# Five small moves in the attention half of a fused attention and feed-forward kernel

## The chip, the cores and the metric

The kernel runs on one core of one Trainium2 chip. The metric is the device time of one launch in microseconds (us). The core has five engines that run side by side, each through its own list of instructions in order, and wait for each other by semaphores: TensorE (PE; its weight loads are shown as PEld), VectorE (DVE), ScalarE (ACT), GpSimd (POOL) and SyncE (SP), which here does nothing but issue DMA transfers. TensorE writes to PSUM, and DVE and ACT read it from there.

## The reference

```python
scores = q @ k.T / 8 + bias[head]          # 4 batches, 8 heads, 576 x 576, head size 64
attn = exp(scores - max); attn = attn / (sum(attn) + 1e-9)
x = (attn @ v) as (2304, 512)
x = max(x @ w1, x @ w2, x @ w3) @ w_out    # 512 -> 768 -> 512
h = x @ w_in                               # 512 -> 2048
out = where(h > 0, h, exp(min(h, 0)) - 1) @ w_out2
```

The bias is a small network of the two positions, one 576 x 576 table per head, the same for all batches. The inputs are 32-bit floats; the weights of the feed-forward parts arrive as 64-bit floats and are taken apart by integer operations on the chip.

## The kernel before

It has three parts. A prologue (to about 56 us) computes the bias tables and writes them to DRAM. The attention part follows (to about 317 us). The rest is the two feed-forward layers, in which TensorE is busy without a break.

The attention part handles 16 pairs n of two heads of one batch. A pair has five steps c: steps 0 to 3 take 128 queries of both heads each, step 4 takes the last 64 queries of both heads at once. So there are 80 steps, s = 5n + c. The steps are staggered: a table of numbers (`OFF`, `PV_AT`, `X_AT`) gives each piece of work of step s a key such as s + 2.10. All pieces are sorted by key, and emitted in that order. I call "slot c" the stretch of keys in which the scores of a step c are made. Keys do not set times: each engine runs its own pieces in the order of their keys as soon as their semaphores allow.

What happens in slot s, on each engine, in order:

- PE: scores of the first head of step s into PSUM tile PB[0] (`unit_qk`, L222), of the second head into PB[1]; then the turning of step s-2 (`trans`, L252), which turns the exponentials of 512 keys per head, in 64 x 64 pieces, into the PSUM tiles TQ[0] and TQ[1] by a matmul with a diagonal matrix of the reciprocal sums; then the tails (`tails`, L252 too), the same for the last 64 keys, into columns at the two ends of PB[0]; then some products with v (`pv`, L319 to L327) into the PSUM tiles XO[0] and XO[1]. Step 4 has one score tile and half as much to turn.
- DVE: `scores` of the first head (L230, reads PB[0], adds the bias, keeps the minimum; its second instruction, READ_ACCUMULATOR, ends it); the sum plus 1e-9 and its reciprocal for step s-1 (L240, L241); `scores` of the second head; the copy of the tails out of PB[0] (L77, `p<-pb`); one operation of the weight decoder (`pump`, L420 to L430; not in slot 1); the copy of TQ[1] for steps 0 and 2, the steps named by `EVD` (L77, `p<-tq`).
- ACT: the exponentials (L235), the other copies of TQ (L75), and the copy of XO[0] (`x_copy`, L341). DVE adds XO[1] to it (`x_sum`, L345).
- POOL: the diagonal matrices (`diag`, L249), one instruction per head, and the split of the result into a high and a low part (L73, L81).
- SP: per pair one load of q and k (`load_kq`, L96, 864 KB), one of v (`load_v`, L100, 320 KB), in every fourth pair nine loads of bias, and about one load of raw weights (L371) and one store of split weights (L466) per pair. Each waits in order until its buffer is free. There are two buffers for q and k, and two for v.

Of the kernel before, what the change touches and what calls it, by code (L numbers as in the profile page):

```python
# [31 lines left out]

OFF = {"qk0": 0.0, "qk1": 0.01, "t0": 0.02, "ns": 1.025, "dg": 1.026, "t1": 0.03, "tr": 2.10, "tl": 2.20, "evt": 2.311,
       "pump": 0.32, "ev0": 2.385, "ev1": 2.387, "ex0": 0.38, "ex1": 0.40}
PV_AT = {1: [(4.5, 0), (4.5, 1), (5.5, 2), (5.5, 3), (5.5, 4)],
         4: [(3.5, 0), (3.5, 1), (4.5, 2), (4.5, 3), (5.5, 4)]}
X_AT = {1: 5.6, 4: 5.6}
EVD = {0, 2}  # L40
# [13 lines left out]
def fused_kernel(ctx, tc, tkq, vv, lt, pk, wm1, wo1, win2, wo2, out):  # L54
    nc = tc.nc
# [29 lines left out]
    tp = att.enter_context(tc.tile_pool(name="tp", bufs=2))  # L85
    sp = att.enter_context(tc.tile_pool(name="sp", bufs=8))
# [3 lines left out]
    kq = att.enter_context(tc.tile_pool(name="kq", bufs=2))  # L90

    KQ, TV = {}, {}

    def load_kq(n):
        KQ[n] = kq.tile([128, 1728], F32, tag="kq", name="kq_t")
        nc.sync.dma_start(KQ[n], tkq[n])  # L96

    def load_v(n):
        TV[n] = ld.tile([128, 640], F32, tag="tv", name="tv_t")
# [21 lines left out]
    with ExitStack() as pro:  # L121
# [18 lines left out]
        with tc.manual_schedule():  # L140
            nc.sync.dma_start(pk_t, pk)
            nc.sync.dma_start(lt_t[:, 512:1148], lt[:, 512:1148])
            nc.sync.dma_start(lt_t[:, 0:512], lt[:, 0:512])
            load_kq(0)
            load_v(0)
            nc.vector.tensor_scalar(nbt, psi_t, b1_t, -1.0, op0=ALU.mult, op1=ALU.mult)
# [32 lines left out]
            for A in range(36):  # L179
# [9 lines left out]
                o = bt.tile([128, 576], F32, tag="o", name="o_t")  # L189
# [5 lines left out]
                c, r = divmod(A, 8)  # L195
# [11 lines left out]
    TQ, XO = [[psp.tile([128, 512], F32, name=f"{n}{i}") for i in range(2)] for n in ("tq", "xo")]  # L207
    PAIR = [(PB[i][:, 0:512], PB[i][:, 512:1024]) for i in (1, 0)] + [tuple(TQ), tuple(XO)]
    ident2 = xp.tile([128, 64], F32, name="ident2")
    nc.vector.tensor_copy(ident2[0:64], ident[0:64, 0:64])  # L210
    nc.vector.tensor_copy(ident2[64:128], ident[64:128, 64:128])
    H64 = [slice(0, 64), slice(64, 128)]
    steps = [(n, c) for n in range(4 * NP) for c in range(5)]
    E, ST, PT = {}, {}, {}
# [19 lines left out]
        e, st = E[s][:, 576 * h:576 * h + 576], ST[s]  # L234
        nc.scalar.activation(e, e, AF.Exp, bias=st[:, h:h + 1], scale=-1.0, accum_out=st[:, 2 + h:3 + h])  # L235

    def recip(s):
        nh = 2 if steps[s][1] < 4 else 1
        st = ST[s]
        nc.vector.tensor_scalar(st[:, 4:4 + nh], st[:, 2:2 + nh], 1e-9, None, op0=ALU.add)  # L240
        nc.vector.reciprocal(st[:, 6:6 + nh], st[:, 4:4 + nh])  # L241

    DG = {}

    def diag(s):
        nh = 2 if steps[s][1] < 4 else 1
        DG[s] = sp.tile([128, 2, 64], F32, tag="dg", name="dg_t", bufs=3)
        for h in range(nh):
            nc.gpsimd.tensor_scalar(DG[s][:, h], ident2, ST[s][:, 6 + h:7 + h], 1.0, op0=ALU.mult, op1=ALU.mult)  # L249

    def flip(dst, s, g, h, k0):
        mm(dst, E[s][H64[g], k0:k0 + 64], DG[s][H64[g], h % nheads(s)], start=True, stop=True)  # L252

    def nheads(s):
        return 2 if steps[s][1] < 4 else 1
# [14 lines left out]
            for h in range(2):  # L270
                flip(x[h][0:64], s, h, 0, 512)

    def trans(s):
        n, c = steps[s]
        if c == 0:
            PT[n, 0] = [tp.tile([128, 8, 256], F32, tag="pa", name="p0", bufs=1)]
        elif c == 2:
            PT[n, 1] = [tp.tile([128, 8, 320], F32, tag="pc", name="p1", bufs=1)]
        if c in (0, 2):
            PT[n, c // 2].append(tp.tile([128, 256], F32, tag="p3", name="p3", bufs=3))  # L280
        elif c == 4:
            PT[n, 1].append(tp.tile([64, 128], F32, tag="p4", name="p4", bufs=1))
        for h in range(nheads(s)):
            for k in range(4):
                for g in range(2):
                    for kh in range(2):
                        col = 256 * h + 64 * k
                        flip(TQ[g][H64[kh], col:col + 64], s, g, h, 576 * h + 128 * k + 64 * kh)
# [41 lines left out]
    XF = {}  # L330

    def x_where(s):
        n, c = steps[s]
        hp, b = divmod(n, 4)
        w, t0 = (256, b * S) if c == 1 else (320, b * S + 256)
        return XH[:, hp, t0:t0 + w], XL[:, hp, t0:t0 + w], w

    def x_copy(s):
        w = x_where(s)[2]
        XF[s] = tp.tile([128, 320], F32, tag="xf", name="xf", bufs=1)[:, 0:w]  # L340
        nc.scalar.activation(XF[s], XO[0][:, 0:w], AF.Copy)  # L341

    def x_sum(s):
        w = x_where(s)[2]
        nc.vector.tensor_tensor(out=XF[s], in0=XO[1][:, 0:w], in1=XF[s], op=ALU.add)  # L345

    def x_hi(s):
        hi_of("p", x_where(s)[0], XF[s])
# [199 lines left out]
    def at(key, fn, *args):  # L548
        plan.append((key, len(plan), fn, args))

    for s, (n, c) in enumerate(steps):
        o = {nm: s + off for nm, off in OFF.items()}
        at(o["qk0"], unit_qk, s, 0)
        at(o["t0"], scores, s, 0)
        at(o["ex0"], expo, s, 0)
        if c < 4:
            at(o["qk1"], unit_qk, s, 1)
            at(o["t1"], scores, s, 1)
            at(o["ex1"], expo, s, 1)
# [139 lines left out]
    def small(tag, bufs):  # L699
        return mp.tile([128, NB], F32, tag=tag, name=f"{tag}_t", bufs=bufs)  # L700
# [61 lines left out]
    with tc.manual_schedule():  # L762
        for n, u in enumerate(units + [None]):
# [6 lines left out]
            if n < 2:  # L770

                for i in range(2):
                    w = take_w(("wi", u[1], 3 * i))
                    v = take_w(("w3", pre[1], i)) if pre else None
                    for q, (b, d) in enumerate(((B11, B21), (B12, B22))):
# [3 lines left out]
                        c = small("c", 4)  # L779
# [14 lines left out]
            w = take_w(("wi", u[1], 0))  # L794
# [11 lines left out]
            w = take_w(("wi", u[1], 1))  # L806
# [11 lines left out]
            w = take_w(("wi", u[1], 2))  # L818
# [10 lines left out]
            w = take_w(("wi", u[1], 3))  # L829
# [71 lines left out]
```

## Time and profile before

| | us |
|---|---|
| median of 3 runs (1012.16 to 1016.56) | 1013.38 |
| the profiled execution | 1010.22 |
| its span from the first to the last instruction | 1008.4 |
| PE busy in the span | 977.4 (97%) |
| DVE, ACT, POOL busy | 692.1, 526.1, 341.7 |

The profile is of one execution. Its times count from the start of the span. A busy PE can still be a PE that has waited, since the ends of matmuls are modelled: two starts far apart tell more than a small idle time. "<- X" names what an idle engine waited for; "issue" is idle time in which it waited for nothing that the profile shows.

### The profile page before, as it was taken

How to read it: one execution, taken by the hardware profiler on the slowest of the kernel's cores; microseconds unless marked ns; L12 is line 12 of the kernel's file. 1: busy time of each engine (PE TensorE's matmuls, PEld its weight loads, DVE VectorE, ACT ScalarE, POOL GpSimd, SP SyncE). 2: the span in 40 equal slices, each digit the busy share in tenths (PEclk: the TensorE clock that was granted, in tenths of full speed). 3: DMA queues.
4: the chain of work that ended last, by engine and by line, in shares of the span. 5: the costliest groups of instructions: out<-in, count | busy, mean ns of one | idle time of the engine just before them, and what ended most of it. 6: DMA issues, size and time to landing. Idle time of an engine off the chain costs nothing.

```text
span 1008.4 us, 28525 instructions
## 1 busy us (share of the span) xinstructions
PE 977.4 (97%) x11748; PEld 869.2 (86%) x11748; DVE 692.1 (69%) x1428; ACT 526.1 (52%) x1087; POOL 341.7 (34%) x419
## 2 busy tenths in 40 slices
PE   7979899999999999999999999999999999999998
PEld 4447777778887899999999999998998989988996
DVE  7967778788886699887887862835574355743342
ACT  8967777777775233333333331644445344453443
POOL 0013344344343354534553550323232132321222
PEclk9989999999999999999999999999999999999999
DMA  7842724645532356879886981355657556575553
GB/s 259 291 172 85 247 94 157 205 163 187 176 127 79 134 187 215 308 234 341 321 282 236 328 298 47 116 189 175 199 192 252 191 171 204 188 258 185 176 197 105
DMA packets 65905, 201.00 MB, mean 199 GB/s; under 512 B 7024, under 2 KB 14832, under 8 KB 65776
## 3 DMA queue, kind: packets, MB, share of 16 engines
q1 hardware_dynamic: 65776, 199.18, 57.6%
q8 instruction: 93, 1.52, 0.6%
q14 instruction: 36, 0.29, 0.1%
HBM read 150.78 MB, written 48.37 MB: 197 GB/s over the span
## 4 chain that ended last, share of the span: by engine, by line
PE 91%; DVE 6%; issue 1%; DMA 1%; ACT 0%; SPq 0%; POOL 0%; DVEq 0%; POOLq 0%; ACTq 0%
PE xo L696 18%; PE pb L740 13%; PE pb L526 12%; PE tq L740 6%; PE tq L252 6%; PE xo L319 6%; PE xo L526 5%; PE tq L526 5%; PE pb L222 5%; PE pb L620 4%; PE pb L183 3%; PE pbb L183 2%; DVE e_t L230 2%; PE xo L620 2%; PE tq L620 2%
## 5 line engine op out<-in xcount | busy, mean ns | idle before, releaser
L81 POOL TENSOR_TENSOR gl<-t_t,gh 128x384 fp32r<-128x384 f32 x96 | 108.7, 1142 | 286.3 <-ACT gh L75 286.3
L235 ACT ACTIVATE e_t<-e_t,st_t 128x576 f32<-128x576 f32 x144 | 111.4, 773 | 58.6 <-DVE st_t L240 56.1
L230 DVE CUSTOM_DVE_ANT_0 e_t<-pb,b_t 128x576 f32<-128x576 f32 x144 | 107.7, 749 | 32.7 <-PE pb L222 32.5
L249 POOL TENSOR_SCALAR dg_t<-ident,st_t 128x64 f32<-128x64 f32 x144 | 48.1, 348 | 212.7 <-DVE st_t L241 93.2
L740 PE MATMUL pb<-w_t,gh 128*128 128x512 f32 x384 | 119.3, 392 | 0.0
L526 PE MATMUL pb<-xh,w_t 128*128 128x384 f32 x448 | 116.8, 336 | 0.0
L252 PEld LDWEIGHTS tq<-dg_t,e_t 64*64 64x64 f32 x4608 | 96.6, 136 | 22.7 <-issue 7.7
L252 PE MATMUL tq<-dg_t,e_t 64*64 64x64 f32 x4608 | 97.8, 222 | 10.9 <-issue 5.3
L696 PE MATMUL xo<-tt,w_t 128*128 128x384 f32 x528 | 107.4, 338 | 0.0
L718 ACT ACTIVATE t_t<-c_t 128x384 f32<-128x384 f32 x96 | 50.0, 521 | 103.4 <-DVE c_t L709 95.6
L222 PE MATMUL pb<-kq_t 64*64 64x288 f32 x1152 | 98.6, 413 | 3.8 <-issue 1.3
L696 PEld LDWEIGHTS xo<-tt,w_t 128*128 128x128 f32 x528 | 95.0, 188 | 7.7 <-issue 0.3
L696 PE MATMUL xo<-xh,w_t 128*128 128x384 f32 x328 | 94.6, 335 | 0.0
L319 PE MATMUL xo<-p,tv_t 64*64 64x320 f32 (+1 forms) x1024 | 85.4, 408 | 1.6 <-issue 1.2
L526 PEld LDWEIGHTS pb<-xh,w_t 128*128 128x128 f32 x448 | 81.1, 188 | 0.5 <-issue 0.4
L740 PEld LDWEIGHTS pb<-w_t,gh 128*128 128x128 f32 x384 | 70.5, 188 | 6.6
L740 PE MATMUL pb<-w_t,gl 128*128 128x512 f32 x192 | 75.5, 393 | 0.0
L526 PE MATMUL pb<-xl,w_t 128*128 128x384 f32 x224 | 75.3, 336 | 0.0
L75 ACT ACTIVATE p<-tq 128x512 f32<-128x512 f32 (+1 forms) x128 | 62.8, 528 | 16.4 <-PE tq L252 15.2
L222 PEld LDWEIGHTS pb<-kq_t 64*64 64x64 f32 x1152 | 50.9, 133 | 22.9 <-DVE p L77 4.4
L75 ACT ACTIVATE gh<-t_t 128x384 fp32r<-128x384 f32 x96 | 48.6, 519 | 33.4 <-DVE t_t L726 33.4
L696 PEld LDWEIGHTS xo<-xh,w_t 128*128 128x128 f32 x328 | 60.2, 188 | 3.0
(131 smaller groups left out, 2198.1 us busy)
## 6 DMA issues: line engine op xcount, KB each, us to landing
w_t<-scw_w SPq DMA_DIRECT2D x90, 512.0 KB, 4.4
w_t<-scw_wi SPq DMA_DIRECT2D x74, 512.0 KB, 4.2
kq_t<-tkq SPq DMA_DIRECT2D x16, 864.0 KB, 5.4
scw_wi<-sp SPq DMA_DIRECT2D x26, 512.0 KB, 4.7
scw_w<-sp SPq DMA_DIRECT2D x22, 512.0 KB, 5.5
raw<-wo SPq DMA_DIRECT2D x22, 512.0 KB, 3.7
scr<-o_t SPq DMA_DIRECT2D x36, 288.0 KB, 3.9
raw<-wm SPq DMA_DIRECT2D x18, 512.0 KB, 4.1
```

The source lines that it names most:

```text
L75: nc.scalar.activation(dst, src, AF.Copy)
L81: e.tensor_tensor(out=dst, in0=src, in1=hi.bitcast(F32), op=ALU.subtract)
L183: mm(p[32 * a4:32 * a4 + 32, 224 + 288 * hf:512 + 288 * hf], w28, FT[A, a4][:, 288 * hf:288 * hf + 288], start=True, stop=True)
L222: mm(PB[h][H64[g], 224 + 288 * r:512 + 288 * r], t[H64[r], 576 + 576 * a + q0:640 + 576 * a + q0], t[H64[r], 288 * a:288 * a + 288], start ...
L230: nc.vector.tensor_tensor_reduce(out=E[s][:, 576 * h:576 * h + 576], in0=PB[h][:, 224:800], in1=BT[n // 4, c, h], op0=ALU.add, op1=ALU.min ...
L235: nc.scalar.activation(e, e, AF.Exp, bias=st[:, h:h + 1], scale=-1.0, accum_out=st[:, 2 + h:3 + h])
L252: mm(dst, E[s][H64[g], k0:k0 + 64], DG[s][H64[g], h % nheads(s)], start=True, stop=True)
L319: mm(XO[g][H64[h], 0:w], v[H64[g], 128 * k + 64 * h:128 * k + 64 * h + 64], ps[0][H64[g], 4 * h + k, :], start=(k == 0), stop=(k == 3 and ...
L526: mm(ps[blk][:, 0:NB], wt[:, ks], xt[:, kk, t0:t0 + NB], start=(j == 0), stop=(j == 11))
L620: mm(ps[blk][:, 0:NB], WO[0][:, kk, wt, ms], xt[:, bs], start=(j == 0), stop=(j == 3 * NM1 - 1))
L696: mm(ps, w[wt][:, ks], b[xt][:, kk], start=(start and j == 0), stop=(stop and j == 5), skip_group_check=True)
L740: mm(acc[t], g[:, ts], w[k], start=(f == 0 and i == 0 and j == 0), stop=(f == NU - 1 and i == 1 and j == 2))
```

## The change

Five edits, all in the attention part.

1. `diag` makes both diagonal matrices of a step in one VectorE instruction, right behind the reciprocal, instead of one GpSimd instruction per head.
2. `x_copy` copies XO[0] and also XO[1] on ACT, and `x_sum` adds the two copies on GpSimd.
3. `trans` is split by head, and `tails` stands between the two halves (keys 2.10, 2.11, 2.12, where the tails had 2.20). Step 4 has the first half alone.
4. The load of q and k becomes three of 288 KB each (k; q of the first head; q of the second) at keys one step apart, and all loads of q, k and v have keys one step later.
5. `EVD` has step 3 too: its copy of TQ[1] moves from ACT to DVE.

```diff
-OFF = {"qk0": 0.0, "qk1": 0.01, "t0": 0.02, "ns": 1.025, "dg": 1.026, "t1": 0.03, "tr": 2.10, "tl": 2.20, "evt": 2.311,
+OFF = {"qk0": 0.0, "qk1": 0.01, "t0": 0.02, "ns": 1.025, "t1": 0.03, "tr0": 2.10, "tl": 2.11, "tr1": 2.12, "evt": 2.311,
-EVD = {0, 2}
+EVD = {0, 2, 3}
...
-    def load_kq(n):
-        KQ[n] = kq.tile([128, 1728], F32, tag="kq", name="kq_t")
-        nc.sync.dma_start(KQ[n], tkq[n])
+    def load_kq(n, i=None):
+        if not i:
+            KQ[n] = kq.tile([128, 1728], F32, tag="kq", name="kq_t")
+        cs = slice(576 * i, 576 * i + 576) if i is not None else slice(0, 1728)
+        nc.sync.dma_start(KQ[n][:, cs], tkq[n][:, cs])
...
-        DG[s] = sp.tile([128, 2, 64], F32, tag="dg", name="dg_t", bufs=3)
-        for h in range(nh):
-            nc.gpsimd.tensor_scalar(DG[s][:, h], ident2, ST[s][:, 6 + h:7 + h], 1.0, op0=ALU.mult, op1=ALU.mult)
+        d = DG[s] = sp.tile([128, 2, 64], F32, tag="dg", name="dg_t", bufs=3)
+        nc.vector.tensor_tensor(out=d[:, 0:nh], in0=ident2.unsqueeze(1).to_broadcast([128, nh, 64]),
+                                in1=st[:, 6:6 + nh].unsqueeze(2).to_broadcast([128, nh, 64]), op=ALU.mult)
...
-        XF[s] = tp.tile([128, 320], F32, tag="xf", name="xf", bufs=1)[:, 0:w]
-        nc.scalar.activation(XF[s], XO[0][:, 0:w], AF.Copy)
+        XF[s] = [tp.tile([128, 320], F32, tag=f"xf{i}", name="xf", bufs=1)[:, 0:w] for i in range(2)]
+        for i in range(2):
+            nc.scalar.activation(XF[s][i], XO[i][:, 0:w], AF.Copy)
...
-        nc.vector.tensor_tensor(out=XF[s], in0=XO[1][:, 0:w], in1=XF[s], op=ALU.add)
+        nc.gpsimd.tensor_tensor(out=XF[s][0], in0=XF[s][0], in1=XF[s].pop(), op=ALU.add)
+        XF[s] = XF[s][0]
...
-        at(o["ns"], recip, s)
-        at(o["dg"], diag, s)
-        at(o["tr"], trans, s)
+        at(o["ns"], diag, s)
+        at(o["tr0"], trans, s, 0)
+        if c < 4:
+            at(o["tr1"], trans, s, 1)
         at(o["tl"], tails, s)
...
-        at(5 * n + 0.2, load_kq, n + 1)
-        at(5 * n + 6.2, load_v, n + 1)
+        for i in range(3):
+            at(5 * n + 1.2 + i, load_kq, n + 1, i)
+        at(5 * n + 7.2, load_v, n + 1)
```

TensorE's order at the tails of a full step: `tq_859` and `tq_860` are TQ[0] and TQ[1], `pb_99` is PB[0]. Before, the end of the turning, the tails, and the products with v:

```order
L252 MATMUL tq_859<-dg_t,e_t 64x64 x2
L252 MATMUL tq_860<-dg_t,e_t 64x64 x2
L252 MATMUL tq_859<-dg_t,e_t 64x64 x2
L252 MATMUL tq_860<-dg_t,e_t 64x64 x2
L252 MATMUL pb_99<-dg_t,e_t 64x64 [waits DVE_49]
L252 MATMUL pb_99<-dg_t,e_t 64x64 x3
L323 MATMUL xo_861<-p_1688,tv_t 64x256
L323 MATMUL xo_862<-p_1688,tv_t 64x256
```

And now, at the same step (of the second half of the turning the first four rows are shown):

```order
L251 MATMUL tq_859<-dg_t,e_t 64x64 x2
L251 MATMUL tq_860<-dg_t,e_t 64x64 x2
L251 MATMUL pb_99<-dg_t,e_t 64x64 [waits DVE_49]
L251 MATMUL pb_99<-dg_t,e_t 64x64 x3
L251 MATMUL tq_859<-dg_t,e_t 64x64 x2
L251 MATMUL tq_860<-dg_t,e_t 64x64 x2
L251 MATMUL tq_859<-dg_t,e_t 64x64 x2
L251 MATMUL tq_860<-dg_t,e_t 64x64 x2
```

The tails, with their wait for DVE, have moved ahead of the 16 turnings of the second head.

SP's order around the loads for one pair of heads, before (`kq_t` is q and k, `tv_t` is v):

```order
L371 DMA raw<-wm 128x1024 [waits DMAHW4_49,DVE_49]
L96 DMA kq_t<-tkq 128x1728 [waits DMAHW5_49,PE_49]
L100 DMA tv_t<-vv 128x640 [waits DMAHW6_49,PE_49]
L466 DMA scw_w_0_2_2681<-w_t 128x1024 [waits DMAHW7_49,Pool_49]
L96 DMA kq_t<-tkq 128x1728 [waits DMAHW1_49,DMAHW0_49,PE_49]
```

And now:

```order
L372 DMA raw<-wm 128x1024 [waits DMAHW6_49,DVE_49]
L98 DMA kq_t<-tkq 128x576 [waits DMAHW7_49,PE_49]
L102 DMA tv_t<-vv 128x640 [waits DMAHW0_49,PE_49]
L98 DMA kq_t<-tkq 128x576 [waits DMAHW1_49]
L98 DMA kq_t<-tkq 128x576 [waits DMAHW2_49]
L467 DMA scw_w_0_2_2688<-w_t 128x1024 [waits DMAHW3_49,Activation_49,Pool_49]
```

The first third of q and k and the load of v wait for PE; the two other thirds come right behind them in SP's list and wait for earlier transfers alone.

## Rows read from the trace of the kernel before

**Rows 1.** Stretches: busy us of PE, PEld, DVE, ACT, POOL; PE clock, DMA share, GB/s.
```profile
64.00:317.00 253.00, 237.69 (x7317) 198.13 (x7319) 206.35 (x628) 189.90 (x453) 99.65 (x210) 0.99 0.44 151
317.00:1008.00 691.00, 685.78 (x3805) 645.21 (x3798) 431.71 (x667) 280.60 (x552) 240.71 (x202) 1.00 0.62 211
```

**Rows 2.** Waits of PE, 62 to 330 us: us in total, times, longest.
```profile
PE tq L252 <- issue: 5.3, 7, 1.7
...
PE pb L252 <- issue: 1.7, 2, 1.2
PE pb L252 <- DVE st_t L230: 1.3, 5, 0.6
PE pb L222 <- issue: 1.3, 1, 1.3
...
PE xo L319 <- issue: 1.2, 2, 0.7
```

**Rows 3.** Timeline of PE, pair 13 into 14: start, us, instruction, [idle before].
```profile
277.73 0.22 PE L252 MATMUL pb<-dg_t,e_t 64*64 64x64 f32 x1
...
280.99 0.23 PE L252 MATMUL pb<-dg_t,e_t 64*64 64x64 f32 x2
...
282.19 0.76 PE L222 MATMUL pb<-kq_t 64*64 64x288 f32 x8
282.67 1.20 PE L252 MATMUL tq<-dg_t,e_t 64*64 64x64 f32 x64
283.83 0.34 PE L252 MATMUL pb<-dg_t,e_t 64*64 64x64 f32 x8
...
286.54 0.30 PE L252 MATMUL pb<-dg_t,e_t 64*64 64x64 f32 x8
...
289.60 0.27 PE L252 MATMUL pb<-dg_t,e_t 64*64 64x64 f32 x2 [0.21 <-DVE st_t L230]
```

**Rows 4.** Timeline of DVE over the same steps.
```profile
277.31 0.08 DVE L230 DVE_READ_ACCUMULATOR2_ANT st_t<- 128x1 f32 x1
...
280.65 0.08 DVE L230 DVE_READ_ACCUMULATOR2_ANT st_t<- 128x1 f32 x1
...
283.01 0.76 DVE L230 CUSTOM_DVE_ANT_0 e_t<-pb,b_t 128x576 f32<-128x576 f32 x1 [0.53 <-PE pb L222]
283.69 0.08 DVE L230 DVE_READ_ACCUMULATOR2_ANT st_t<- 128x1 f32 x1
...
286.06 0.09 DVE L230 DVE_READ_ACCUMULATOR2_ANT st_t<- 128x1 f32 x1
...
287.59 1.28 DVE L423 TENSOR_SCALAR t_w<-raw 128x512 int32<-128x512 int32 x1
```

**Rows 5.** Groups by line, 64 to 317 us: shapes, count | busy us, mean ns.
```profile
L249 POOL TENSOR_SCALAR dg_t<-ident,st_t 128x64 f32<-128x64 f32 x141 | 46.7, 345 | 209.7 <-DVE st_t L241 92.4 <-DVE ident L211 60.4 <-PE pb L252 49.8
...
L77 DVE COPY p<-tq 128x512 f32<-128x512 f32 x31 | 21.1, 682 | 0.0
...
L81 POOL TENSOR_TENSOR xl<-xf,xh 128x320 fp32r<-128x320 f32 x14 | 12.7, 906 | 0.9
...
L345 DVE TENSOR_TENSOR xf<-xo,xf 128x320 f32<-128x320 f32 x14 | 6.6, 472 | 0.0
...
L345 DVE TENSOR_TENSOR xf<-xo,xf 128x256 f32<-128x256 f32 x15 | 6.0, 403 | 0.0
L341 ACT ACTIVATE xf<-xo 128x320 f32<-128x320 f32 x14 | 6.0, 428 | 0.2
```

**Rows 6.** Timeline 119 to 123 us, SP and PE, around one wait for "issue".
```profile
119.90 0.34 SPq L96 DMA_DIRECT2D kq_t<-tkq  x1
...
122.03 0.63 PE L252 MATMUL tq<-dg_t,e_t 64*64 64x64 f32 x28 [1.72 <-issue]
```

**Rows 7.** Stretches with and without transfers; columns as in rows 1.
```profile
114.00:127.00 13.00, 9.74 (x331) 8.21 (x324) 9.10 (x30) 9.80 (x22) 5.13 (x11) 1.00 0.81 268
129.50:138.00 8.50, 8.50 (x274) 7.65 (x268) 6.90 (x22) 6.68 (x18) 3.34 (x8) 1.00 0.02 6
```

More of the change, by code (lines that the diff above doesn't have):

```diff
@@ L235, in expo, with diag @@
         nc.scalar.activation(e, e, AF.Exp, bias=st[:, h:h + 1], scale=-1.0, accum_out=st[:, 2 + h:3 + h])
-    def recip(s):
-        nh = 2 if steps[s][1] < 4 else 1
+    DG = {}
+    def diag(s):
+        nh = nheads(s)
         st = ST[s]
@@ L241, in recip @@
         nc.vector.reciprocal(st[:, 6:6 + nh], st[:, 4:4 + nh])
-    DG = {}
-    def diag(s):
-        nh = 2 if steps[s][1] < 4 else 1
-        DG[s] = sp.tile([128, 2, 64], F32, tag="dg", name="dg_t", bufs=3)
-        for h in range(nh):
-            nc.gpsimd.tensor_scalar(DG[s][:, h], ident2, ST[s][:, 6 + h:7 + h], 1.0, op0=ALU.mult, op1=ALU.mult)
+        d = DG[s] = sp.tile([128, 2, 64], F32, tag="dg", name="dg_t", bufs=3)
+        nc.vector.tensor_tensor(out=d[:, 0:nh], in0=ident2.unsqueeze(1).to_broadcast([128, nh, 64]),
+                                in1=st[:, 6:6 + nh].unsqueeze(2).to_broadcast([128, nh, 64]), op=ALU.mult)
     def flip(dst, s, g, h, k0):
@@ L271, in tails, with trans @@
                 flip(x[h][0:64], s, h, 0, 512)
-    def trans(s):
+    def trans(s, h):
         n, c = steps[s]
-        if c == 0:
+        if h:
+            pass
+        elif c == 0:
             PT[n, 0] = [tp.tile([128, 8, 256], F32, tag="pa", name="p0", bufs=1)]
@@ L278, in trans @@
             PT[n, 1] = [tp.tile([128, 8, 320], F32, tag="pc", name="p1", bufs=1)]
-        if c in (0, 2):
+        if h == 0 and c in (0, 2):
             PT[n, c // 2].append(tp.tile([128, 256], F32, tag="p3", name="p3", bufs=3))
-        elif c == 4:
+        elif h == 0 and c == 4:
             PT[n, 1].append(tp.tile([64, 128], F32, tag="p4", name="p4", bufs=1))
[L283 to L288, printed above, removed]
+        for k in range(4):
+            for g in range(2):
+                for kh in range(2):
+                    col = 256 * h + 64 * k
+                    flip(TQ[g][H64[kh], col:col + 64], s, g, h, 576 * h + 128 * k + 64 * kh)
     def evac(s, g):
@@ L339, in x_copy @@
         w = x_where(s)[2]
-        XF[s] = tp.tile([128, 320], F32, tag="xf", name="xf", bufs=1)[:, 0:w]
-        nc.scalar.activation(XF[s], XO[0][:, 0:w], AF.Copy)
+        XF[s] = [tp.tile([128, 320], F32, tag=f"xf{i}", name="xf", bufs=1)[:, 0:w] for i in range(2)]
+        for i in range(2):
+            nc.scalar.activation(XF[s][i], XO[i][:, 0:w], AF.Copy)
     def x_sum(s):
-        w = x_where(s)[2]
-        nc.vector.tensor_tensor(out=XF[s], in0=XO[1][:, 0:w], in1=XF[s], op=ALU.add)
+        nc.gpsimd.tensor_tensor(out=XF[s][0], in0=XF[s][0], in1=XF[s].pop(), op=ALU.add)
+        XF[s] = XF[s][0]
     def x_hi(s):
```

## The prediction

> **What bounds the kernel now.** I read the stretches first. After 317 us TensorE is busy for 685.78 of 691 us, so nothing that this change touches can be won there. In the attention part, 64 to 317 us, PE is busy 237.69 of 253 us, DVE 206.35, ACT 189.90, POOL 99.65 [rows 1]. PE sets the pace, with DVE not far behind. So an edit counts if it adds a wait to PE or takes one away, and work that moves between DVE, ACT and POOL counts only where PE then waits for it.
>
> Second, PE's own waits [rows 2]. The largest kind is "issue": 5.3 + 1.7 + 1.3 + 1.2 = 9.5 us in 12 waits, during which no engine is late. That is the most that the new order of loads can give back. Waits for data are small: 1.3 us at the tails for DVE's scores.
>
> Third, the timelines of PE and DVE through one pair [rows 3, 4]. What the reader is to see is which score instruction the tails wait for. In slot 4 the scores of the first head end at 283.69 + 0.08 = 283.77, and the tails start at 283.83. In slot 1 the row of the tails names DVE's score as what PE waited for. In no slot do the tails start before that end plus about 0.05 us. The tails go into PB[0], and the scores read PB[0]. So the tails of step s-2 wait for the first scores of step s, which came two pieces earlier in the order. Before, the whole turning (0.98 us from first start to last: 1.20 less one matmul's own 0.22) covers that wait.
>
> **Part 1: the tails between the halves.** PE works in order, so the second half of the turning now stands behind the tails and their wait. The half takes 0.49 us. If nothing else moved, a slot would be later by 0.49 less the spare time that the tails had before, which is their start minus (end of the scores + 0.05):
> - slot 2: 277.73 - (277.39 + 0.05) = 0.29 spare, cost 0.20;
> - slot 3: 280.99 - (280.73 + 0.05) = 0.21 spare, cost 0.28;
> - slot 4: 283.83 - (283.77 + 0.05) = 0.01 spare, cost 0.48;
> - slot 0: 286.54 - (286.15 + 0.05) = 0.34 spare, cost 0.15;
> - slot 1 turns step 4, which has one half alone: no cost.
>
> Sum 1.11 us a pair. But the slots feed each other. In slot 3 part of the small spare comes from DVE being late; if PE is later by slot 2's 0.20, DVE has caught up. The scores then come at a fixed distance behind their matmuls, as in slot 4, where DVE sat idle for them (0.53 us): 283.01 - 282.19 = 0.82, plus 0.76 for the scores and 0.05, so 1.63 us after the start of the score matmuls. PE by then has made two score tiles (0.48 each, 282.19 to 282.67) and half of the turning: 0.96 + 0.49 = 1.45. It waits 0.18. I take 0.18 for slots 3 and 0 both. Pair: 0.20 + 0.18 + 0.48 + 0.18 = 1.04. In slot 4 there is one score tile only, so PE arrives after 0.48 + 0.49 = 0.97 and waits 0.66 less the little it waited before; the way by the spare time says 0.48, which I keep.
>
> Fifteen pairs run like this (the first is filling up): 15.6 us. Bounds: 7.2 us if slot 4 alone pays (15 x 0.48), and 16.7 us with the costs of the list (15 x 1.11). PE waits nowhere later in the pair for something that this would make earlier, so I see nothing that gives the time back.
>
> **Part 2: DVE, ACT and POOL.** `diag` on DVE is not in the trace. The nearest rows are the additions of 256 and 320 columns, 403 and 472 ns [rows 5]; 64 columns are 69 ns, so 128 columns come to about 0.27 us and 64 to 0.20. That is an estimate from PSUM operands; the ends I keep are 0.08 (the read of an accumulator, the shortest DVE row) and 0.40. A pair: +4 x 0.27 + 0.20 = 1.28, less x_sum 0.40 + 0.47, plus the third copy 0.68: DVE gains 1.1 us in a pair of 15.8 (253 / 16), of which it is busy 12.9 (206.35 / 16). PE's new waits cover that in slots 2, 3, 4. Not in slot 0, where the third copy falls: behind the weight decoder's operation (1.28 us at worst, for one decoder step in five) and ahead of slot 1's scores, for which PE waited 0.21 already [rows 3, 4]. There DVE gains 0.68 + 0.20 - 0.47 = 0.41 for that worst operation. The shorter ones leave room. I take 0.1 a pair, 1.5 us; bounds 0 and 0.41 x 15 = 6. ACT gains two copies a pair near the 0.43 us of its row and loses one copy of TQ[1]: hidden, since it is busy 189.90 of 253 us. POOL loses 46.7 us and gains 32 additions, near the 0.91 us of its row for two SBUF operands: hidden behind two slots of slack. If ACT's second copy of XO were late, the next products with v would wait; PE has a slot between, so I take 0. In the first pair, DVE now waits for the identity before its second scores, instead of after; tails and copies come earlier in the two slots behind it. I set it to 0, within 1.5 either way.
>
> **Part 3: the loads.** Twelve waits for "issue" cost 9.5 us. One, of 1.72 us, starts right after a load of q and k is issued [rows 6], and between 114 and 127 us, with DMA at 0.81, PE is idle 3.26 us; between 129.5 and 138, with DMA at 0.02, it is idle for none [rows 7]. So I read these waits as late instructions that queue behind data. [...]
>
> Does the change spread the loads? The keys do, but SP's order shows the second and third part right behind the load of v, waiting for nothing of the moment. SP runs ahead. Only the first third comes earlier, by the wait of v's buffer; 320 + 576 = 896 KB still leave in one go, where 864 left before. In every fourth pair the loads of bias, which wait for DVE, do part them. So a quarter to a third of 9.5: I take -2.5 us; bounds 0 and -9.5.
>
> **Sum.** 15.6 + 1.5 + 0 - 2.5 = +14.6 us on the profiled 1010.22, or 1024.8. The median of the runs lies 3.2 us above that execution, which would give 1028.0; I put the changed kernel between the two, at 1026. Ends: 7.2 - 9.5 - 1.5 = -4 and 16.7 + 6 + 1.5 = +24, so 1009 to 1038 on the median.
>
> **Rivals.**
> 1. *The instructions' lateness is the real brake, and the smaller loads cure it.* All 9.5 us go. For the kernel to become faster, the tails' wait must then cost under 4.4 us. That holds if the first scores of each step end some 0.3 us sooner against the turning, so that slot 4 alone pays, in part. For it: the waits are the largest kind on PE. Against it: in slot 4 DVE sits idle for the matmul, so nothing can make the scores sooner. Time: 1013.4 - 9.5 + 3.6 (half of slot 4's cost) = 1007.5. Chance 0.10.
> 2. *Half and half: slot 4 alone pays in full, and the loads give 4 us.* 1013.4 + 7.2 - 4 = 1016.6, within what can be told from no change. For it: the spare times of 0.2 to 0.34 us are near to half of the turning, so a small gain in DVE's order would close them. Against it: `diag` makes DVE later, not sooner. Chance 0.18.
> 3. *DVE becomes the pace.* With 1.1 us more a pair and slot 1's scores behind the third copy, every pair pays the 0.41 in slot 1 (6 us), and all slots pay the costs of the list (16.7 us), with 1.5 for the first pair: 1013.4 + 24 = 1037. For it: DVE is at 206.35 of 253. Against it: most decoder operations are half of the longest one. Chance 0.10.
> 4. *The change doesn't do what it says:* that the loads are not spread is in my forecast. If they were, the forecast would be 2 to 6 us lower; that is inside the range.
>
> **How the numbers follow.** My forecast, 1019 to 1034, has 0.62; rival 1 0.10, rival 2 0.18, rival 3 0.10. A measurement of this kernel can tell about 0.5%, 5 us, from no change. So faster 0.10, same 0.18, slower 0.62 + 0.10 = 0.72. The range that leaves out 2 in 10, one on each side, is 1012 to 1035.
>
> **What would show it.** PE's wait at the tails (PB[0], line 251) for the scores' accumulator should grow from 1.3 us to over 10 us, most in slot 4, about 0.6 us a time, and the mean time of a pair from 15.8 to 16.7 us. PE's busy share of the attention part falls. The waits for "issue" should still stand at the loads of q and k. The second half of the turning should start within 0.2 us of the tails. I am wrong if the tails start right behind the first half, without a wait; if pairs stay at 15.8 us; or if the "issue" waits are gone and the loads of q and k land one slot apart.

## The result, and the profile after

| | before | changed |
|---|---|---|
| median of 4 runs each, us | 1012.77 (1009.14 to 1016.56) | 1027.80 (1027.19 to 1028.26) |
| the profiled execution, and its span | 1010.22, 1008.4 | 1027.19, 1025.1 |

The ratio is 1.0148, with a 95% interval of 1.011 to 1.0186: slower by 15 us. All but some 2 us of the 16.7 between the two spans lies in the attention part. First the stretches of the changed kernel, with the columns of [rows 1]; the attention part now ends near 332 us, where it ended near 317.

```profile
64.00:332.00 268.00, 246.89 (x7268) 183.31 (x7272) 235.68 (x697) 198.19 (x469) 73.35 (x98) 0.99 0.44 142
332.00:1025.00 693.00, 686.76 (x3871) 646.38 (x3860) 432.09 (x671) 282.15 (x556) 241.04 (x202) 1.00 0.62 211
```

PE was idle for 15.3 us before and for 21.1 now, so idle time tells little more than a third of the story; the rest hides in a busy PE. DVE went from 206 of 253 us to 236 of 268: 29 us more, where the prediction's 1.1 us a pair makes 18. The waits of PE, 62 to 335 us (total, times, longest):

```profile
PE pb L251 <- DVE st_t L232: 6.8, 16, 0.4
PE tq L251 <- DVE p L77: 6.1, 12, 1.4
PE pb L224 <- DVE st_t L232: 5.1, 1, 5.1
PE pb L224 <- DVE p L77: 3.9, 16, 0.7
PE xo L319 <- issue: 2.2, 3, 1.0
PE tq L251 <- issue: 0.8, 2, 0.4
```

Against [rows 2]: the wait of the tails grew from 1.3 to 6.8 us, waits for "issue" fell from 9.5 to 3.0, and two waits for DVE's copies grew, from 2.4 to 6.1 us at the turning and from 1.2 to 3.9 us at the next scores. All 16 waits at the tails stand in slot 4, one in each pair.

Since the rows can show PE busy through a wait (slot 4 of the kernel before: 0.16 us, first experiment), I measure slots by starts: from the first score matmul of a slot to that of the next, as the median over pairs 1 to 14. The mean of a pair less the sum of its medians collects what strikes a few slots only, such as late instructions. "15 pairs" is the trace's distance from the first score matmul of pair 0 to that of pair 15. Each row is read from one execution, and executions of one kernel lie up to 10 us apart (1004.8 to 1014.5 for the kernel before on one chip), so the last two columns are less sure than the medians. One execution of "diagonal back" took 4399 us, and its ratio below leaves that out.

| us | slot 0 | 1 | 2 | 3 | 4 | sum | mean pair | 15 pairs |
|---|---|---|---|---|---|---|---|---|
| before | 3.40 | 3.03 | 3.36 | 3.26 | 2.40 | 15.45 | 16.21 | 244.3 |
| changed | 3.17 | 3.83 | 3.71 | 3.58 | 2.63 | 16.92 | 17.25 | 259.6 |
| tails back | 3.28 | 3.72 | 3.71 | 3.36 | 2.41 | 16.48 | 17.13 | 258.2 |
| diagonal back | 3.27 | 3.05 | 3.69 | 3.44 | 2.74 | 16.20 | 16.87 | 253.7 |
| third copy back | 3.17 | 3.24 | 3.70 | 3.59 | 2.63 | 16.34 | 16.94 | 255.4 |
| sum back | 3.46 | 3.92 | 3.42 | 3.97 | 2.63 | 17.40 | 17.64 | 265.3 |
| loads back | 3.18 | 3.83 | 3.71 | 3.59 | 2.63 | 16.93 | 17.59 | 265.0 |
| decoder moved (on changed) | 3.17 | 3.09 | 3.72 | 3.58 | 2.63 | 16.18 | 17.08 | 257.5 |
| tails alone | 3.19 | 3.01 | 3.58 | 3.35 | 2.63 | 15.77 | 16.80 | 251.8 |
| diagonal alone | 3.67 | 3.32 | 3.47 | 3.74 | 2.41 | 16.62 | 16.80 | 254.4 |
| diagonal alone, late | 3.75 | 3.74 | 3.46 | 4.00 | 2.40 | 17.35 | 17.85 | 267.6 |
| loads alone | 3.40 | 3.00 | 3.36 | 3.26 | 2.48 | 15.51 | 16.49 | 248.6 |
| sum alone | 3.06 | 3.29 | 3.41 | 3.48 | 2.51 | 15.74 | 16.22 | 245.2 |
| decoder moved (on before) | 3.40 | 2.93 | 3.38 | 3.31 | 2.60 | 15.62 | 16.26 | 245.6 |

From before to changed: every pair costs 1.47 us more in its medians, 20.6 over 14 pairs; what strikes a few slots fell by 0.43 a pair, -6.0 over 14; the first pair is 0.7 longer (17.4 to 18.1). Together 15.3, the difference over 15 pairs.

### The profile page after: what moved, and what is told of

Its sections match the earlier page's. It is cut to its first block, busy times and chain, and to the rows that moved or that the text cites. A ratio compares the mean times of both kernels' runs of the same rounds, so it can differ in the third digit from the quotient of the medians.

```text
span 1025.1 us, 28405 instructions
## 1 busy us (share of the span) xinstructions
PE 986.9 (96%) x11748; PEld 854.7 (83%) x11748; DVE 719.4 (70%) x1492; ACT 534.3 (52%) x1103; POOL 315.4 (31%) x307
## 4 chain that ended last, share of the span: by engine, by line
PE 85%; DVE 12%; issue 1%; DMA 1%; ACT 0%; SPq 0%; DVEq 0%; ACTq 0%
PE xo L699 17%; PE pb L743 13%; PE pb L527 11%; PE tq L743 6%; PE xo L527 5%; PE tq L527 5%; DVE e_t L232 5%; PE pb L224 4%; PE tq L251 4%; PE xo L319 4%; PE pb L623 4%; PE pb L185 3%; PE pbb L185 2%; DVE p L77 2%; PE xo L623 2%; PE tq L623 2%
## 5 line engine op out<-in xcount | busy, mean ns | idle before, releaser
L81 POOL TENSOR_TENSOR gl<-t_t,gh 128x384 fp32r<-128x384 f32 x96 | 108.7, 1142 | 286.2 <-ACT gh L75 286.2
L251 PE MATMUL tq<-dg_t,e_t 64*64 64x64 f32 x4608 | 104.6, 221 | 7.4 <-DVE p L77 6.1
L345 POOL TENSOR_TENSOR xf<-xf 128x256 f32<-128x256 f32 (+1 forms) x32 | 25.5, 798 | 257.6 <-ACT xf L342 257.6
L224 PE MATMUL pb<-kq_t 64*64 64x288 f32 x1152 | 91.4, 417 | 9.9 <-DVE st_t L232 5.9
L319 PE MATMUL xo<-p,tv_t 64*64 64x320 f32 (+1 forms) x1024 | 78.6, 406 | 2.3 <-issue 2.2
L224 PEld LDWEIGHTS pb<-kq_t 64*64 64x64 f32 x1152 | 42.2, 133 | 41.7 <-DVE p L77 22.6
L75 ACT ACTIVATE p<-tq 128x512 f32<-128x512 f32 (+1 forms) x112 | 56.3, 531 | 10.6 <-PE tq L251 10.6
```

What stands on the lines that cost most here:

```text
L81: e.tensor_tensor(out=dst, in0=src, in1=hi.bitcast(F32), op=ALU.subtract)
L224: mm(PB[h][H64[g], 224 + 288 * r:512 + 288 * r], t[H64[r], 576 + 576 * a + q0:640 + 576 * a + q0], t[H64[r], 288 * a:288 * a + 288], start ...
L319: mm(XO[g][H64[h], 0:w], v[H64[g], 128 * k + 64 * h:128 * k + 64 * h + 64], ps[0][H64[g], 4 * h + k, :], start=(k == 0), stop=(k == 3 and ...
```

## The experiments

Each undoes one edit of the changed kernel, or makes one edit alone in the kernel before. The ratio is to the kernel before on the same chip. The changed kernel itself was not timed beside them, so a difference of two ratios is uncertain by 0.4 to 0.5%, or 4 to 5 us; the traces' slots decide where it does not suffice.

**Tails alone**, on the kernel before.
```diff
-at(o["tr"], trans, s)           # tr 2.10, tl 2.20
+at(o["tr0"], trans, s, 0)       # tr0 2.10, tl 2.11, tr1 2.12
+if c < 4:
+    at(o["tr1"], trans, s, 1)
```


> The kernel before with the tails between the halves alone. Theory A: 15.6 us slower than before, 1027. Theory C: with DVE no busier than before, PE's waits at the tails cost 1.04 us a pair only where PE was the pace; 5 to 10 us slower, 1016 to 1021. Moving the tails back in the changed kernel gave 5 us; if one alone costs 15, the costs of the edits overlap and don't add.

Measured: 1018.86 us, ratio 1.0079 (1.0059 to 1.0099). The medians cost 0.32 us a pair, not 1.04. PE's wait at the tails, from this kernel's waits, and slot 4 of one pair on PE:

```profile
PE pb L251 <- DVE st_t L232: 7.7, 22, 0.5
```
```profile
207.81 0.67 PE L224 MATMUL pb<-kq_t 64*64 64x288 f32 x8
208.29 0.64 PE L251 MATMUL tq<-dg_t,e_t 64*64 64x64 f32 x32
209.36 0.34 PE L251 MATMUL pb<-dg_t,e_t 64*64 64x64 f32 x8 [0.42 <-DVE st_t L232]
...
209.99 0.38 PE L323 MATMUL xo<-p,tv_t 64*64 64x256 f32 x1
...
210.43 0.47 PE L224 MATMUL pb<-kq_t 64*64 64x288 f32 x3
```

The wait that I predicted stands there. But the kernel before had a wait of its own behind the same tails, which its rows show as a busy PE. First PE, then DVE, of the kernel before, in slot 4 of pair 13:

```profile
283.99 0.38 PE L323 MATMUL xo<-p,tv_t 64*64 64x256 f32 x1
...
284.59 1.20 PE L222 MATMUL pb<-kq_t 64*64 64x288 f32 x16
```
```profile
284.24 0.29 DVE L77 COPY p<-pb 128x128 f32<-128x128 f32 x1 [0.19 <-PE pb L252]
```

The next scores write PB[0], so they wait for DVE's copy of the tails out of it: 284.24 + 0.29 = 284.53, and they start at 284.59, 0.60 us behind the first product with v. With the tails earlier, the copy is done before PE has finished the same products: 210.43 - 209.99 = 0.44. That gives back 0.16 of the 0.48; another 0.09 comes from scores that end sooner (tails 1.55 us behind the slot's start, 1.64 before). Beside its slots, this trace has two stretches of 3.4 us at a granted clock of 0.50, from 77.8 and from 125.6 us, behind waits for "issue" of 1.9 and 1.7 us; the traces before and changed have none after 70 us.

**Tails back**, in the changed kernel.
```diff
-"tr0": 2.10, "tl": 2.11, "tr1": 2.12
+"tr0": 2.10, "tl": 2.13, "tr1": 2.12
```


> The changed kernel with the tails behind both halves of the turning again; the other four edits stay. Theory A (the prediction's sizes: the tails' wait is the cost, 15.6 us): about 15 us faster than the changed kernel, near 1012 to 1013, level with the kernel before. Theory B (read from the changed kernel's trace: the third copy, which holds up slot 1, and the sum on GpSimd, which blocks DVE, are as large as the tails): 5 to 9 us faster than the changed kernel, 1019 to 1023. In both, PE's waits at the tails for the scores fall back to 1 to 2 us.

Measured: 1022.53 us, ratio 1.0113 (1.0089 to 1.0138). Slots 3 and 4 return to within 0.1 of before, slot 2 does not move (3.71): DVE sets it now. From slot 2's first scores on DVE to slot 3's the median is 3.99 us with the tails in either place, and 3.36 in the kernel before. The sum falls by 0.44 a pair, but the waits for "issue" come back (7.8 us), with one stretch of 3.4 us at a clock of 0.50 behind the longest of them, so that the 15 pairs of the trace gain only 1.4.

**Diagonal alone**, on the kernel before.
```diff
-nc.gpsimd.tensor_scalar(DG[s][:, h], ident2, ST[s][:, 6 + h:7 + h], 1.0, ...)
+nc.vector.tensor_tensor(out=d[:, 0:nh], in0=ident2..., in1=st[:, 6:6 + nh]..., op=ALU.mult)
```


> The kernel before with the diagonals on DVE alone. Theory A: 0 to 2 us slower than before, 1011 to 1013. Theory C: 6 to 12 us slower, 1017 to 1023, with 1 us of it in the first pair, and with new waits of the score matmuls for the copy of the tails out of PB[0].

Measured: 1020.49 us, ratio 1.0115 (1.0089 to 1.0141): at least as dear as the tails, where my 1.5 stood for all of VectorE's work, with the sum's relief counted against it. The sum grows by 1.17 a pair, 0.48 of it in slot 3, 0.27 and 0.29 in slots 0 and 1, 0.11 in slot 2. DVE from slot 0's first scores to slot 1's:

```profile
208.15 0.75 DVE L232 CUSTOM_DVE_ANT_0 e_t<-pb,b_t 128x576 f32<-128x576 f32 x1
...
209.20 0.23 DVE L247 TENSOR_TENSOR dg_t<-ident,st_t 128x64 f32<-128x64 f32 x1
209.34 0.48 DVE L345 TENSOR_TENSOR xf<-xo,xf 128x320 f32<-128x320 f32 x1
...
210.62 1.28 DVE L423 TENSOR_SCALAR t_w<-raw 128x512 int32<-128x512 int32 x1
211.82 0.74 DVE L232 CUSTOM_DVE_ANT_0 e_t<-pb,b_t 128x576 f32<-128x576 f32 x1
```

Not one row of this stretch has an idle time ahead of it. DVE's list is full here, though over a whole pair DVE has idle time left, and what is added is paid.

**Diagonal back**, in the changed kernel.
```diff
-nc.vector.tensor_tensor(out=d[:, 0:nh], in0=ident2..., in1=st[:, 6:6 + nh]..., op=ALU.mult)
+for h in range(nh):
+    nc.gpsimd.tensor_scalar(d[:, h], ident2, st[:, 6 + h:7 + h], 1.0, ...)
```


> The changed kernel with the diagonals on GpSimd again, one instruction per head; the other four edits stay. Theory A (the tails' wait is the cost, the diagonal hides): 0 to 2 us faster than the changed kernel, near 1026. Theory C (after the first four experiments: DVE is the pace, and what stands between its first and second scores is paid in full): the second scores start some 0.3 us sooner in the slots with a diagonal, so 8 to 14 us faster, 1014 to 1020; PE's wait for the scores at 60 to 65 us (5.1 us in the changed kernel) is gone, which is 1 us of it.

Measured: 1021.47 us, ratio 1.0093 (1.0072 to 1.0114), just short of Theory C's 1014 to 1020; the 15 pairs fall by 5.8. Slot 1 goes from 3.83 to 3.05, the value of before, with the third copy still in it.

**Diagonal alone, late**: as the diagonal alone, with the sum, the reciprocal and the diagonal behind the copy of the tails.
```diff
-"ns": 1.025
+"ns": 1.312
```


> The kernel before with the diagonals on DVE, but together with the sum and the reciprocal behind the copy of the tails instead of between the first and the second scores. Theory C1 (DVE's list is full from slot 2's first scores to slot 3's, and from slot 0's to slot 1's; any work added there is paid, wherever it stands): 7 to 11 us slower than before, as with the diagonals in their place (10 us). Theory C2 (only what stands ahead of the second scores and the tails' copy is paid): 0 to 3 us slower than before. Theory A (DVE's work hides): 0 to 1 us.

Measured: 1032.26 us, ratio 1.021 (1.0188 to 1.0232), dearer than ahead of the second scores, and twice what Theory C1 gave. This kernel's waits of PE (62 to 345 us):

```profile
PE tq L251 <- DVE p L77: 13.1, 28, 0.7
PE tq L251 <- DVE dg_t L247: 5.7, 6, 4.0
```

The turning waits for the copy of TQ[1], which the late diagonal pushes back. So it is not only the place ahead of the second scores that costs; the list has no gap at either place. Part of the difference between the places is another thing: at the late one, subtractions on GpSimd hold up these operations (one ended at 209.62, and the sum plus 1e-9 that had started at 209.09 ended at 209.64, after 0.55 us; last section), and the diagonal of one head takes 0.45 us at the mean, against 0.23 in "diagonal alone", the sum plus 1e-9 0.26 against 0.19.

**Third copy back**, in the changed kernel.
```diff
-EVD = {0, 2, 3}
+EVD = {0, 2}
```


> The changed kernel with the copy of TQ[1] of step 3 back on ACT; the other four edits stay. Theory A (third copy and diagonal together 1.5 us): 1025 to 1027. Theory B: slot 1 is 0.7 to 0.85 us a pair shorter, so 10 to 13 us faster than the changed kernel, 1015 to 1018; the waits of the turning for DVE's copy (6.1 us in the changed kernel) fall to about 2 us.

Measured: 1023.07 us, ratio 1.0118 (1.0094 to 1.0142), not Theory B's 1015 to 1018; the 15 pairs fall by 4.2. Slot 1 goes to 3.24 and no other slot moves by more than 0.01. PE's wait at the turning for DVE's copy falls from 6.1 to 2.6 us.

**Decoder moved (on changed)**: the one decoder operation of slot 0 runs in slot 1.
```diff
-if s > 5 and c != 1:
+if s > 5 and c != 0:
```


> The changed kernel with the weight decoder's operation of slot 0 moved to slot 1, where DVE sits idle for PE; all five edits stay. Theory A (the tails' wait is the cost): 0 to 2 us faster than the changed kernel. Theory C1 (DVE is full from slot 0's first scores to slot 1's, since the third copy stands there too): slot 0 to 1 loses 0.5 to 0.8 us a pair, so 7 to 12 us faster, 1016 to 1021.

Measured: 1023.12 us, ratio 1.0124 (1.0102 to 1.0146), not Theory C1's 1016 to 1021, though slot 1 goes to 3.09 as it said. DVE around the third copy, in the changed kernel and then in this one:

```profile
213.01 0.76 DVE L232 CUSTOM_DVE_ANT_0 e_t<-pb,b_t 128x576 f32<-128x576 f32 x1 [0.23 <-PE pb L224]
...
215.21 1.18 DVE L424 TENSOR_SCALAR t_w<-raw 128x512 int32<-128x512 int32 x1
216.31 0.68 DVE L77 COPY p<-tq 128x512 f32<-128x512 f32 x1
216.91 0.74 DVE L232 CUSTOM_DVE_ANT_0 e_t<-pb,b_t 128x576 f32<-128x576 f32 x1
```
```profile
215.18 0.28 DVE L77 COPY p<-pb 128x128 f32<-128x128 f32 x1
215.38 0.67 DVE L77 COPY p<-tq 128x512 f32<-128x512 f32 x1
216.30 0.76 DVE L232 CUSTOM_DVE_ANT_0 e_t<-pb,b_t 128x576 f32<-128x576 f32 x1 [0.24 <-PE pb L224]
```

With the operation gone DVE waits for PE again, 0.24 us, and slot 1 is TensorE's. The diagonal, the third copy, the decoder operation: taking away any one of three cures slot 1, or most of it. The sum falls by 0.74 a pair, yet the 15 pairs by 2.1 only: the mean stands 0.90 above the sum, where the changed kernel has 0.33, and the waits for "issue" are 7.1 us again.

**Decoder moved (on before)**: the same edit there.

> The kernel before with the decoder's operation of slot 0 moved to slot 1. If PE is the pace there: the same as before. Theory C1 (DVE is full in slot 0 already, and PE waits 0.2 us at the tails of slot 1 for it): 1 to 4 us faster than before, 1007 to 1010.

Measured: 1012.41 us, ratio 1.0025 (1.0002 to 1.0048): hardly to be told from no change, and not the 1 to 4 us faster of Theory C1. Slot 1 gains 0.10, slot 4 loses 0.20; I did not follow slot 4's loss to its cause.

**Sum alone**, on the kernel before.
```diff
-nc.vector.tensor_tensor(out=XF[s], in0=XO[1][:, 0:w], in1=XF[s], op=ALU.add)
+for i in range(2):
+    nc.scalar.activation(XF[s][i], XO[i][:, 0:w], AF.Copy)
+nc.gpsimd.tensor_tensor(out=XF[s][0], in0=XF[s][0], in1=XF[s].pop(), op=ALU.add)
```


> The kernel before with the second copy on ACT and the sum on GpSimd alone. Theory A: nothing, within 1 us. Theory C1: DVE loses 0.40 and 0.47 us a pair in its full stretches, but in slot 2 its sum-plus-1e-9 is held for 0.5 us by the sum on GpSimd: slot 0 to 1 is 0.3 shorter, slot 2 to 3 is 0.2 longer, so 0 to 4 us faster than before.

Measured: 1011.38 us, ratio 1.0013 (0.9996 to 1.0029). Slot 0 gains 0.34, slots 1 and 3 lose 0.48 together.

**Sum back**, in the changed kernel: the reverse of that edit.

> The changed kernel with the sum of the two products back on DVE, from one copy; the other four edits stay. Theory A (moving work off DVE hides or helps): DVE has 0.87 us a pair more to do, so the same or up to 5 us slower than the changed kernel, 1028 to 1033. Theory B (the sum on GpSimd holds DVE's tiny sum-plus-1e-9 for 0.71 instead of 0.16 us in slot 2): that row is 0.16 again and the kernel 0 to 5 us faster, 1023 to 1028.

Measured: 1033.22 us, ratio 1.0215 (1.019 to 1.024); the 15 pairs grow by 5.7. Theory B, which had it faster, is wrong: in company the edit is worth its work on DVE, alone it is worth nothing. It may also cost something: with the sum back on DVE slot 2 falls from 3.71 to 3.42, but slot 3 grows from 3.58 to 3.97, so no run parts the cost from the relief. The tiny operation that adds 1e-9, by its group in the kernel before (64 to 317 us), the changed one (to 332) and this one (to 335):

```profile
L240 DVE TENSOR_SCALAR st_t<-st_t 128x2 f32<-128x2 f32 x62 | 10.1, 162 | 0.0
```
```profile
L244 DVE TENSOR_SCALAR st_t<-st_t 128x2 f32<-128x2 f32 x62 | 19.5, 315 | 0.3 <-ACT e_t L237 0.3
```
```profile
L244 DVE TENSOR_SCALAR st_t<-st_t 128x2 f32<-128x2 f32 x61 | 11.9, 195 | 0.3 <-ACT e_t L237 0.3
```

It takes twice its time in the changed kernel, and most of the excess is gone when the sum is back on DVE (last section).

**Loads alone**, on the kernel before.
```diff
-at(5 * n + 0.2, load_kq, n + 1)
-at(5 * n + 6.2, load_v, n + 1)
+for i in range(3):
+    at(5 * n + 1.2 + i, load_kq, n + 1, i)
+at(5 * n + 7.2, load_v, n + 1)
```


> The kernel before with the loads of q and k in three and the later keys alone. Theory A: 2.5 us faster than before, 1008 to 1009. Theory B and C: 6 to 8 us faster, 1003 to 1005, with PE's waits for 'issue' at 3 us or less instead of 9.5. If the longer slots of the changed kernel covered the late fetches, and not the loads: the same as before.

Measured: 1014.26 us, ratio 1.0034 (1.002 to 1.0049): slightly slower, where I had -2.5. The medians do not move (15.51 against 15.45); the mean does, by 0.28 a pair. The waits for "issue" are 12.6 us, not less than the 9.5 of before. The longest, on PE, and what came after it:

```profile
122.76 0.63 PE L254 MATMUL tq<-dg_t,e_t 64*64 64x64 f32 x28 [3.09 <-issue]
...
123.96 2.16 PE L224 MATMUL pb<-kq_t 64*64 64x288 f32 x16
```

**Loads back**, in the changed kernel: the reverse of that edit, with one load of 864 KB.

> The changed kernel with one load of 864 KB for q and k and the old keys of the loads; the other four edits stay. Theory A (the loads give 2.5 us): 1030 to 1031. Theory B (they give 6 us: PE's waits for 'issue' fell from 9.5 to 3.0 us): 1032 to 1036, with waits for 'issue' of 7 us and more again. If the longer steps alone covered the fetches, the time stays at 1028 and the waits at about 3 us.

Measured: 1035.74 us, ratio 1.0243 (1.0219 to 1.0267). Here the new loads are worth 8 us by the medians of the runs and 5.5 by the 15 pairs. Every slot's median is that of the changed kernel to 0.01, so the whole difference is in a few slots and the first pair (18.8 us). PE's waits in this kernel:

```profile
PE xo L319 <- issue: 5.1, 3, 2.1
PE pb L224 <- issue: 2.5, 2, 1.9
PE tq L251 <- issue: 1.1, 3, 0.5
```

8.7 us against 3.0: the 5.7 us between them are of the size of the 5.5.

No kernel here beats the one before; the sum alone is level with it, and the decoder moved on before within half a percent.

## Why the prediction was right, and by which errors

The time was right, 1026.0 against 1027.8, and so was the direction. The terms were not: the one I was sure of was too large, the one I called hidden was as large as it, and they made up for each other. That the sum came within 2 us is luck.

**Part 1, 15.6 us: right mechanism, half the size.** The tails do wait for the scores, 7.7 us in 22 waits with the tails alone, and slots 2, 3 and 4 lengthen. Of the signs I named, the wait at the tails came to 6.8 us in the changed kernel and not to over 10, at 0.42 us a time and not 0.6; the pair went from 16.2 to 17.2 us by its starts, where I had 15.8 to 16.7. Alone the edit costs 8.0 us by the ratio, of which 0.32 x 15 = 4.8 are in the medians; the rest is in a few long slots, and its trace has the two stretches at a clock of 0.50 there. By slot, predicted and measured: slot 2 0.20 and 0.22; slot 3 0.18 and 0.09; slot 4 0.48 and 0.23; slot 0 0.18 and -0.21; slot 1 0 and -0.02. The step that failed is "PE waits nowhere later in the pair for something that this would make earlier". In slot 4 the next scores waited for the copy of the tails, and the rows hid it in the products with v. Slot 0's gain I can't explain: no experiment parts it. Undone in company the edit gives 1.4 us (15 pairs) to 5.3 (medians), less than alone, since DVE then sets slots 1 and 2 whatever the tails do.

**Part 2, 1.5 us: the step "PE's new waits cover that" failed.** The durations were near, but for one: 0.31 us for two heads against 0.27, and 0.68 for the copy; the diagonal of one head took 0.35 against 0.20, held up by GpSimd (last section), and 0.23 with the diagonal alone. The cover was not there. I compared DVE's busy time of a pair, 12.9 of 15.8, where the question was whether its list has a gap between one slot's scores and the next. From slot 2's to slot 3's it has none. DVE in the changed kernel, and in the kernel before:

```profile
203.03 0.76 DVE L232 CUSTOM_DVE_ANT_0 e_t<-pb,b_t 128x576 f32<-128x576 f32 x1 [0.84 <-PE pb L224]
...
203.72 0.71 DVE L244 TENSOR_SCALAR st_t<-st_t 128x2 f32<-128x2 f32 x1
204.46 0.17 DVE L245 RECIPROCAL st_t<-st_t 128x2 f32<-128x2 f32 x1
204.66 0.37 DVE L247 TENSOR_TENSOR dg_t<-ident,st_t 128x128 f32<-128x128 f32 x1
204.95 0.74 DVE L232 CUSTOM_DVE_ANT_0 e_t<-pb,b_t 128x576 f32<-128x576 f32 x1
...
207.03 0.74 DVE L232 CUSTOM_DVE_ANT_0 e_t<-pb,b_t 128x576 f32<-128x576 f32 x1
```
```profile
276.62 0.76 DVE L230 CUSTOM_DVE_ANT_0 e_t<-pb,b_t 128x576 f32<-128x576 f32 x1 [1.11 <-PE pb L222]
277.31 0.16 DVE L240 TENSOR_SCALAR st_t<-st_t 128x2 f32<-128x2 f32 x1
277.50 0.17 DVE L241 RECIPROCAL st_t<-st_t 128x2 f32<-128x2 f32 x1
277.58 0.40 DVE L345 TENSOR_TENSOR xf<-xo,xf 128x256 f32<-128x256 f32 x1
...
279.98 0.75 DVE L230 CUSTOM_DVE_ANT_0 e_t<-pb,b_t 128x576 f32<-128x576 f32 x1
```

Start to start 4.00 us against 3.36, with no idle time inside either. The rows were there before I predicted: slots 3 and 1 began without a wait for PE. By starts, the 0.64 is 0.55 for the held TENSOR_SCALAR (0.74 to the reciprocal, 0.19 before), 0.29 for the diagonal and 0.12 behind the reciprocal, less 0.32 for the sum. What I wrote of rival 3 happened in part, in the stretches 2 to 3 and 0 to 1 and not as the 24 us in all that I gave it: undoing the diagonal gives 5.8 us, undoing the third copy 4.2, both over 15 pairs. Its price for the third copy (0.41 a pair in slot 1) was nearer than the forecast's 0.1; the trace says 0.59 (3.83 less 3.24). The sum on GpSimd, which I counted on the credit side, is worth 5.7 in company.

**First pair, 0 within 1.5:** 0.7 longer. DVE waits 4.0 us to copy the identity ahead of its second scores, and PE waits 5.1 us for DVE, the one large wait for scores in its list; in the kernel before it waited 3.0 us for GpSimd's diagonal there instead.

**Part 3, -2.5 us: within its bounds in company, of the wrong sign alone.** In the changed kernel the waits for "issue" fell by 6.5 us, and undoing the loads costs 5.5 to 8; alone the same edit costs 3.4. That these waits are late instructions holds: each ended 2.2 to 2.7 us after an instruction packet had started (last section). Of my reading of SP's order half held. SP in the changed kernel, for one pair (L102 is v, L98 q and k):

```profile
114.40 0.38 SPq L102 DMA_DIRECT2D tv_t<-vv  x1
114.83 0.42 SPq L98 DMA_DIRECT2D kq_t<-tkq  x1
117.90 0.43 SPq L98 DMA_DIRECT2D kq_t<-tkq  x1
```

The second third does leave right behind v. The third waits for an earlier transfer, and for 8 of the 14 pairs loaded in the attention part it left 2.6 to 3.9 us later, for the others 0.5: it is spread more than I said. I take it that every edit moves the time at which PE needs a packet of instructions, and so which transfer the packet meets; no run parts this. The runs show how large these waits can be and where they stand; why one version meets more of them than another stays open.

**The parts do not add.** Three edits alone give 8.0 + 11.6 + 3.4 by their ratios, the sum on GpSimd 1.3: 24 us, against 15, without the third copy, which no run has alone. Two reasons show in the table. A slot is as long as the longer of two lists, so what PE and DVE lose in slots 2 and 3 is in part paid once: 0.31 us with the tails alone and 0.59 with the diagonal alone, but 0.67 in the changed kernel. And what strikes few slots tends to be less where pairs are longer: 0.33 us a pair in the changed kernel, 0.24 with the sum back, but 0.76 before and 1.03 with the tails alone. It is not a rule (loads back 0.66), and each of these is one execution.

## What to carry to other kernels

Ask of each stretch between two waits whether an engine's list has a gap there; a busy share of 82% over a pair said nothing on the two stretches that had none. Before you say that a delay is not given back, look at the starts of the next work that reads or overwrites the same buffer, since the rows can show an engine busy through a wait, as PE in slot 4 of the kernel before (0.60 us from the first product with v to the next scores, and 0.44 with the tails alone). And take an edit out of the changed kernel as well as putting it into the old one: here the loads changed sign and the sum went from nothing to 6 us between the two.

## What the runs showed of the hardware

**A GpSimd operation held a tiny VectorE operation.** The sum on GpSimd beside the held TENSOR_SCALAR of 203.72:

```profile
203.67 0.73 POOL L345 TENSOR_TENSOR xf<-xf 128x256 f32<-128x256 f32 x1 [4.77 <-ACT xf L342]
```

It ended at 204.40, and the operation of two columns (128x2), usually 0.16 us, at 204.43. Of the 80 such operations in the changed kernel 18 took over 0.25 us. All 18 have two columns, and every one had started while a GpSimd addition or subtraction was running (L345 in 15, L81 in 3). Thirteen others started while L345 had over 0.6 us to go, and took their usual time; all of them have one column, as the last step of a pair has:

```profile
L244 DVE TENSOR_SCALAR st_t<-st_t 128x1 f32<-128x1 f32 x15 | 2.2, 149 | 0.0
```

None that met no GpSimd operation took over 0.25 us. In the kernel before four met one, two of one column and two of two columns with under 0.2 us of it left, and none took over 0.25 us. Each of the 18 ended 0.02 to 0.03 us behind the end of the GpSimd operation that it met, so that the one of 203.72 took 0.55 us more than usual and others up to 0.69. Why the form of two columns is held and that of one is not, no run here shows. In the stretch of 203.03, which has no gap, the 0.55 us stood in front of the next scores on DVE. The diagonal of one head was held too: in the changed kernel 14 of them started during L345, and every one ended 0.08 us after it, mostly at 0.33 us in place of 0.23.

**Late instructions come behind data.** The DMA part of the profile lists queues of their own for instructions, as shares of the same 16 engines; the changed kernel, 64 to 332 us (packets, MB, share):

```profile
q1 hardware_dynamic: 15472, 37.10, 42.4%
q8 instruction: 57, 0.93, 1.5%
```

The packets of q8 have 16,384 bytes, one for every 255 instructions of PE and PEld in this stretch. The waits for "issue" end behind them: each of the 12 before and of the 5 in the changed kernel ended 2.2 to 2.7 us after one of these packets had started. In the 3 us ahead of that packet the data queue took 0.5 to 1.0 of the 16 engines, in all of these cases but one (a wait of 0.35 us); its mean over the attention part of the changed kernel is 0.42.

The longest wait, of 3.09 us, came while the transfers were close to full. "Loads alone" around it, with the columns of [rows 1]:

```profile
117.00:121.00 4.00, 2.67 (x99) 2.43 (x92) 2.03 (x8) 3.37 (x9) 0.77 (x3) 1.00 1.05 399
121.00:124.00 3.00, 1.24 (x50) 1.06 (x49) 0.39 (x2) 0.58 (x1) 0.08 (x1) 1.00 0.82 200
124.00:127.40 3.40, 3.40 (x76) 2.53 (x78) 2.89 (x9) 1.93 (x5) 0.98 (x3) 0.51 0.56 170
```

**A lower granted clock stood behind some of these waits.** Behind that one TensorE's granted clock was 0.51 for 3.4 us, and sixteen score matmuls took 2.16 us in place of 1.20. The kernel with the loads back showed the same at 80.7 to 84.1 us, behind a wait of 2.11 us. Not every long wait is followed by it: behind one of 2.31 us in "loads alone", which ended at 189.83, the granted clock stayed at 1.00. What lowers the clock, no run here shows.
